# Attention and gated expert layer on one core: masks and identity made on the chip, byte-wise third words for ten weight blocks, a new written order, fills in the quieter bank

## The chip, the cores and the metric

The kernel runs on 1 core of one Trainium2 chip. The metric is the device time of one execution in microseconds (us); three executions are given for the kernel before, and one more was recorded by the profiler. Engines are named as the profile does: PE (TensorE matmul), PEld (its weight load), DVE (VectorE), ACT (ScalarE), POOL (GpSimd), SP (SyncE, which issues the DMAs here).

## The reference

```python
# attention: batch 4, heads 8, sequence 768, head size 64; block 32, window 16
k_sum = k.reshape(B, H, nb, block, D).max(axis=3)
v_sum = v.reshape(B, H, nb, block, D).mean(axis=3)
scores_l = scale * np.matmul(q, k.transpose(0, 1, 3, 2))
mask_l = np.abs(pos[:, None] - pos[None, :]) < window
scores_s = scale * np.einsum('bhsd,bhnd->bhsn', q, k_sum) + np.log(block)
scores_all = np.concatenate([np.where(mask_l, scores_l, -1e9), scores_s], axis=-1)
a = np.exp(scores_all - scores_all.max(-1, keepdims=True))
a = a / (a.sum(-1, keepdims=True) + 1e-9)
attn = np.matmul(a, np.concatenate([v, v_sum], axis=2))
# layer on x = attn, heads side by side: batch 4, sequence 768, width 512, inner width 1024
xk = mu_k * x + (1.0 - mu_k) * x_prev      # x_prev: x of the token before
xr = mu_r * x + (1.0 - mu_r) * x_prev
k = np.maximum(xk @ w_k, 0.0)
out = (1.0 / (1.0 + np.exp(-(xr @ w_r)))) * (k * k @ w_v)
```

The weights w_k, w_v and w_r come as 64-bit words (the inputs are 64-bit floats) and are turned into 32-bit floats on the chip; each is then kept as a high and a low part, and a product takes three matmuls (high by high, low by high, high by low).

## The kernel before

**Attention.** A "set" is one batch and one pair of heads (4 x 4 of them), a "unit" is half of the sequence of a set (32 units). `load_set` loads the keys (`kt`, L386; for the first set in two pieces) and the values (`vx`, L391), takes the maxima of key blocks (`kred` L412, `kmax` L416 and L420) and copies them between the windows of `kt` (`kcopy`, L424, on DVE or POOL). For the first batch the means of value blocks go through PE (`vpool` L436, `vsel` L444) and are spread into `vx` by POOL or DVE (`spread`, L450). `unit` loads a query tile (L465), makes the scores (24 small matmuls, L476), adds the mask and takes the minimum of the negated scores in one DVE operation (`mask`, L486, six a unit), takes the exponential (ACT, L490), adds 1e-9 (`eps`), takes the reciprocal, scales (`norm3`, L501 DVE, L507 ACT, L512 POOL), transposes by the identity (PE, L524), copies to SBUF (`pts`, L530 ACT, L532 DVE) and multiplies with the values (L539); the result is copied to `vx` (`evac`, L553 or L554).

**Layer.** `mixes` makes the two blends of a token with the one before and their high and low parts (`mixa` L572 or L575, `mixd` L579, `cast` or `khv` L582 or L584, `sub` L585). `gate` multiplies with w_r (L626 to L628) and takes the sigmoid. For the first half of the first batch it runs by pair of heads (`gate_p`, four operations of nine matmuls). `experts` has `e1` (L655, 12 matmuls for each of eight blocks), relu, square, the split in two parts, and `e2a` and `e2b` (L680, the last block at L706); L712 multiplies by the gate, L716 stores.

**Weights.** Twenty blocks (four of w_r, eight of w_k, eight of w_v), each of 512 KB. `load` (L320) brings the words into one of three `st` tiles; `wscale` (ACT, L327) turns the high words into a float pattern in one of four `wc` tiles; `wshift` (DVE, L331) shifts it left by 3; `wor` (DVE, L335) joins in the upper three bits of the low words; `wcast` (L344 ACT, L346 POOL, L348 DVE) makes the high part and `wsub` (DVE, L349) the low part.

**Constants.** One transfer (L288) brings `fixed_sb`: the three masks of 120 columns, the factors mu, two small selection matrices and the identity of 128 columns, 556 columns in all. `vpool`, `vsel`, the masks, the transposes and the blends all name it as a dependence.

**Order.** All work stands in a list of numbered operations. `ORDER`, a text of 1910 numbers with a letter where an operation goes to another engine than its usual one, says in which order they are issued; each engine works through its own part of that list strictly in turn, SP's queue of transfers too. `Plan.schedule` gives each a planned start from a table of durations (`LENGTH`) and a model of the transfers; these planned starts decide two things only: how many filling matmuls (L753, on a zero tile `still`, into the unused end of the `av` bank) stand ahead of a real PE operation, until the first e1 or gate, and on which DVE operation a POOL operation of the kinds in `SHARED` has to wait.

Of the kernel before, what the change touches and what calls it, by code (L numbers as in the profile page):

```python
# [9 lines left out]
F32 = mybir.dt.float32  # L10
F32R = mybir.dt.float32r
U32 = mybir.dt.uint32
AF = mybir.ActivationFunctionType
ALU = mybir.AluOpType
# [5 lines left out]
BLOCK, WINDOW = 32, 16  # L20
P = 128
# [11 lines left out]
NFIX = 3 * NK + 68 + P  # L33
# [5 lines left out]
LENGTH = dict(  # L39
    score=776, transpose=245, vtrans=30, vpool=800, vsel=320, values=848, mixe=1400, gate=2797, gate_p=2095, e1=2103,  # L40
    e2a=1398, e2b=700, e2=700, e2h=350,
    kred=862, kred2=460, kmax=75, kcopy=225, vred=865, mask=203, eps_d=72, rc=100, norm3=448, evac=470, pts_d=468,
    mixd=530, mixa_d=330, sub=471, psub=472, khv=271, spread=575, wshift=340, wor=605, wsub=605, wcast_d=340,
# [6 lines left out]
    "wor", "wsub", "mixd", "sub", "khv", "kcopy", "eps_d", "kmax", "spread", "wshift", "wcast_d", "norm3", "mixa_d", "diag_d",  # L50
# [5 lines left out]
DMA_FIRST, DMA_ISSUE, DMA_START, DMA_EACH, DMA_END, DMA_BYTES_PER_NS = 740, 470, 900, 100, 1200, 400.0  # L56
FIXED_MORE = 320000
# [5 lines left out]
SPLIT = 0  # L63
BY_PAIR = ((0, 0),)
# [8 lines left out]
245D 376P 399 57 286 246 265D 377 58 619 324 104 585 388 65 93 81 247D 282 278 280 288 266 284 59 60 248 378D 267D 400
82 398 83 379 66 94 269 289 281 279 287 268 74 250A 301 75 270 380 98 348 643 283 285 381 290D 76 271 389 77 78 675
272 84 403 401 308 291 310 302 306 382D 292D 312 309 383 304 105 95 402 404 273 294 325 275A 313 384 390 293 295 385
86 407D 386D 589 387 99 311 307 303 296 297 405 391 408 106 85 409D 107 87 305 108 298 128 586 406 410 314D 88 411 100
89 109 394 96 393 332 315 423 101 317P 328 116 110 412 129 330 334 326 336 413 102 130 316D 97 349 90 414A 318 91 117
416 415 392 319 299A 424 118 131 119 320 421 132P 354 652 759 761 140 594 134 701 588 417D 331 41 321 422 120D 355 337
322 352 590 121 418 335 103 430 111 141 329 419 358 420 112 360 333 327 323A 425 428 142 133 113 135 338 478P 587 122
431D 647 429 474P 350 356 437 339 114 357 479 340D 341D 115 359 426A 432 427 342 361 351 353 143 433A 434 136 435 152  # L80
343 123 436 144 591 362 137 344 363 595 164 345 364 346 145 606 124 598 125 365D 438 366 439 444 599 367D 347A 153
440A 482 602 604 600 126P 644 146 596 79 368 620 369 445 480 127 154 475 370 165 155 442 371A 156 481 483 157 158 677
443 486 441 484D 476 138 607 487 147 488 451 139 605 627 477 485 489 449 452 601 446 453 603 166 167 148 490 705 149
623 150D 631 159 496 597 447A 151 608D 160 450 456 609 161 491 1145 170 577 492 646 625 629 611P 617 454A 504P 500D
501 621 448 497 578 505 614 457 168 162 163 171 493 494 579 615 172 610 648 649P 580 653 495 169 173 763 506 581 735
702 575 612 654 507 656 658 664 791 508P 502 503 455 509 498 630 499 458 510 632 459 626 463 460 461A 624 613 174D 511
464 538 175 576 665 539 659 622 462 582 471 583 465 468 512 628 584 657 704 706 660 633D 634 472 469 517 592 762 466
636P 635D 662 513D 514 540 661 473 703 1149 639 708 1021 710 1023 593 760 650 616 678 515 663 618A 640D 655 839P 637
689 707P 685 709 470 1029 1019 645 768 764 516 679 518 524 522 683 687 666D 681 519 638D 667 817D 520A 521 818 669
819D 820 525D 711 641 672 523 529 722 673D 1022 718 765 840 684 690 686 541 526 688 668 670 527 1148 714 723 680 682  # L90
530 531 528 716 712 642 536 1025 1026 720 532 1033 841 715 671 651 533 545 717 534 721 719 713 535 691D 692 694 724
766 767 1063 1032 736 693D 674 1473 1031 1034 725 467 726P 733 695 676 537 696 737 741 739 738 740 727P 843 697 698D
1035 793 543 745 747 728 743 1150 844 842 546 821 699 742 542 769 700 729 730 1020 780 552 746 744 748 776 772 774
749D 778 547 770 777 731D 750 751D 794 752P 732 1087 553 1476 1088 1147 753 771 554 775 734 544 559 779 1024 1038 1465
795 796 754 845 822 823 781 773 825D 826 548 549 755 797 550 782 824 803 847P 551 801 783 784 560 756D 799 1477 804
798 800 557 555 805 846 1478 561 802 757 806 786 558 827 787 785D 758A 564 807D 808 1151 562 810 788 1039 789 848 556
790 918D 1048 828 813 1050 1091 563 809D 1040 565 919 1044 814 1467 1096 792A 829D 1051 569 566 572 811 1041 1046 1042
830 1090 831D 1064 812 832 815 1045 1043 1089 1205 1027 1049 837 1047 567 851D 849 852 1069 853D 854 1067 1073 1065
1052D 1074 1071 1053 835 570 1055 1028 1075 1054P 573 1237 1153 568 1037 1589 1030 1066 1072 1070 816A 850 1068 1092
1093P 855 1056 1097 1095 926 927 1057D 1058 1121 836 838 574 1211 867 833 1036 1076 1179 930 1108 1109 856 1593 1077D  # L100
1104 1100 1105 857 858 859 1592 834 1098 1078 1106 1079 1080D 1102 1059D 860 861D 1099 1122 862 1107 868D 1060 863 931
1103 869 1081 895 932 1061 1463 1154 1094 865 1125 1062A 1101 864 1082D 1110D 1111 1127 870 1083 866 928 872 896 1594
897 898 920 921 873 874 1112D 1126 1595 922 1128 1133 871 879 875 1129 1464 1123 923 933 880 888 1131 876 877 940 1469
1124 1132 1084D 899 924 941 889D 1130 1119 1155 1085 1212 1114 1177 1113 881 1115 929 878 944 882D 1134 1135 1116 886
1158 1156 925 1166 1167 883 1468 948D 949 934 884 1086A 1159 1157 1160 1204 1117 935 1203 1210 571 887 893 885 945 890
1648 894 891A 936 892 1162 1207 1136 1137 900 937 1164 1206 1208 1209P 1479P 938 1180 1165 942 939 943 1118 1507 1138D
952D 1470 1139 1120A 1146 901 902 1187 1191 953 954D 950D 946D 1235 951 1140D 1265D 947 907 903 904 905A 1188 1163
1141 908 906 1161 955 1287D 1288 1189 912 915 956 1289D 916 1183 1181 1261 1182 1266 1185 957 1142 1262 1267D 1268
# [751 lines left out]
```

## Time and profile before

| | us |
|---|---|
| median of three runs | 445.19 |
| lowest and highest | 444.62, 445.21 |
| the profiled execution | 445.36 |
| its span from the first to the last instruction | 443.6 |
| outside the span | 1.76 |

The profile is one execution. Its page gives the busy time of each engine, 40 slices of the span, the chain of work that ended last and the costliest groups of instructions. Matmuls are pipelined and overlap in the records, so a busy PE is not PE at its peak; the filling matmuls count as busy too. Instructions of DVE and ACT overlap their successors a little as well, so the distance between two starts is shorter than a duration.

### The profile page before, as it was taken

What the parts mean: (1) busy time and instruction counts of PE and PEld (TensorE: products, weight loads), DVE (VectorE), ACT (ScalarE), POOL (GpSimd) and SP (SyncE); (2) the same over time, 40 slices, a digit from 0 to 9 for tenths busy, and PEclk for the clock granted to TensorE, in tenths of its full rate; (3) what the DMA queues carried; (4) which work ended last, traced back from release to release, by engine and by line L of the source; (5) the groups of instructions that cost most, each with busy time, mean ns of one, the idle gap of its engine ahead of it and who ended that gap; (6) DMA issues with size and microseconds to landing.
All of it is one profiled execution on the core that took longest, in us unless ns stands there. A gap on an engine that the chain in (4) does not pass through costs nothing.

```text
span 443.6 us, 9603 instructions
## 1 busy us (share of the span) xinstructions
PE 436.4 (98%) x3582; PEld 375.6 (85%) x3582; DVE 297.1 (67%) x972; ACT 273.3 (62%) x807; POOL 30.9 (7%) x78
## 2 busy tenths in 40 slices
PE   7999999999999999999999999999999999999996
PEld 7877888889888888878898888888888888989885
DVE  3999989998998946648767755557643646444211
ACT  2999999885777597575466666564964315223321
POOL 0140211101030000000000210000000000000000
PEclk9999999999999999999999999999999999999999
DMA  8985868437656170141440143101200010002002
GB/s 309 401 299 194 281 249 265 149 126 227 228 141 253 55 239 27 53 153 55 134 144 19 44 117 105 51 1 42 79 1 1 2 47 1 0 1 95 0 1 95
DMA packets 26878, 51.95 MB, mean 117 GB/s; under 512 B 2512, under 2 KB 14416, under 8 KB 26832
## 3 DMA queue, kind: packets, MB, share of 16 engines
q1 hardware_dynamic: 26832, 51.35, 34.7%
q8 instruction: 28, 0.46, 0.5%
q14 instruction: 18, 0.15, 0.1%
HBM read 43.28 MB, written 6.29 MB: 112 GB/s over the span
## 4 chain that ended last, share of the span: by engine, by line
PE 87%; ACT 5%; DVE 3%; DMA 2%; issue 1%; SPq 0%; DVEq 0%; ACTq 0%
PE mm L655 28%; PE mm L680 25%; PE av L539 5%; PE pt L524 5%; PE sc L476 5%; PE mm L628 4%; PE mm L626 4%; PE mm L627 4%; PE mm L706 4%; PE av L753 2%; ACT y L490 2%; DMA st<-in_w_k 1%; DMA kt<-in_k 1%; DVE y L486 1%; ACT wc L327 1%
## 5 line engine op out<-in xcount | busy, mean ns | idle before, releaser
L655 PE MATMUL mm<-xs,wk_h 128*128 128x384 f32 x512 | 102.0, 341 | 0.6 <-DVE r L663 0.4
L655 PEld LDWEIGHTS mm<-xs,wk_h 128*128 128x128 f32 x512 | 89.5, 188 | 5.7 <-DVE r L663 1.1
L490 ACT ACTIVATE y<-y,mn 128x120 f32<-128x120 f32 x192 | 74.0, 387 | 31.0 <-DVE mn L486 30.8
L680 PE MATMUL mm<-wv_h,kh 128*128 128x512 f32 x168 | 67.2, 400 | 0.0
L680 PE MATMUL mm<-wv_l,kh 128*128 128x512 f32 x168 | 66.3, 395 | 0.0
L655 PE MATMUL mm<-xs,wk_l 128*128 128x384 f32 x256 | 55.3, 337 | 0.0
L665 ACT ACTIVATE r<-r 128x384 f32<-128x384 f32 x64 | 32.7, 520 | 35.0 <-DVE r L663 34.3
L670 DVE TENSOR_TENSOR kl<-r,kh 128x384 fp32r<-128x384 f32 x64 | 35.4, 559 | 26.7 <-ACT kh L669 18.9
L486 DVE CUSTOM_DVE_ANT_0 y<-sc,fixed_sb 128x120 f32<-128x120 f32 x192 | 47.4, 274 | 5.9 <-PE sc L476 3.7
L680 PE MATMUL mm<-wv_h,kl 128*128 128x512 f32 x168 | 49.7, 404 | 0.0
L661 ACT ACTIVATE r<-mm 128x384 f32<-128x384 f32 x42 | 20.5, 489 | 46.2 <-PE mm L655 41.6
L579 DVE SCALAR_TENSOR_TENSOR xa<-vx,fixed_sb,xa 128x384 f32<-128x384 f32 x64 | 39.1, 613 | 10.6 <-ACT xa L572 9.5
L655 PEld LDWEIGHTS mm<-xs,wk_l 128*128 128x128 f32 x256 | 45.6, 188 | 0.0
L585 DVE TENSOR_TENSOR xs<-xa,xs 128x384 fp32r<-128x384 f32 x64 | 35.1, 554 | 5.7 <-ACT xs L582 5.3
L626 PE MATMUL mm<-wr_h,xs 128*128 128x512 f32 x96 | 38.6, 402 | 0.0
L628 PE MATMUL mm<-wr_h,xs 128*128 128x512 f32 x96 | 38.0, 396 | 0.0
L627 PE MATMUL mm<-wr_l,xs 128*128 128x512 f32 x96 | 37.9, 395 | 0.0
L680 PEld LDWEIGHTS mm<-wv_h,kh 128*128 128x128 f32 x168 | 31.6, 188 | 6.2 <-DVE kh L668 0.3
L680 PEld LDWEIGHTS mm<-wv_l,kh 128*128 128x128 f32 x168 | 31.6, 188 | 6.0
L490 ACT ACTIVATION_READ_ACCUMULATOR y<-y,mn 128x1 f32 x192 | 36.3, 189 | 0.0
L680 PEld LDWEIGHTS mm<-wv_h,kl 128*128 128x128 f32 x168 | 30.2, 188 | 5.4
L524 PE MATMUL pt<-fixed_sb,y 128*120 128x128 f32 x192 | 33.2, 282 | 0.0
(76 smaller groups left out, 654.2 us busy)
## 6 DMA issues: line engine op xcount, KB each, us to landing
vx<-in_v SPq DMA_DIRECT2D x32, 384.0 KB
kt<-in_k SPq DMA_DIRECT2D x15, 544.0 KB
qt<-in_q SPq DMA_DIRECT2D x32, 192.0 KB
out<-z SPq DMA_DIRECT2D x23, 256.0 KB
st<-in_vT SPq DMA_DIRECT2D x12, 384.0 KB
st<-in_w_k SPq DMA_DIRECT2D x8, 512.0 KB
st<-in_w_v SPq DMA_DIRECT2D x8, 512.0 KB
st<-in_w_r SPq DMA_DIRECT2D x4, 512.0 KB
```

The source lines that it names most:

```text
L486: op("DVE", "mask", lambda h=h, i=i, var=var: nc.vector.tensor_tensor_reduce(out=y[h].t[:, i, :], in0=sc[h].t[:, i, 0:NK], in1=mask_sb[:, ...
L490: op("ACT", "exp", lambda h=h, i=i: nc.scalar.activation(y[h].t[:, i, :], y[h].t[:, i, :], AF.Exp, bias=mn[h].t[:, i:i + 1], scale=-1.0, a ...
L524: nc.tensor.transpose(out=pt.t[0:NK, i * P:(i + 1) * P], in_=y[h].t[:, i, :], identity=ident_sb)
L579: op("DVE", "mixd", lambda xt=xt, xa=xa, p=p: nc.vector.scalar_tensor_tensor(out=xa.t, in0=xt.t[:, 1 + lo:1 + lo + HT], scalar=mu_sb[:, wh ...
L585: op("DVE", "sub", lambda xa=xa, xh=xh, xl=xl: nc.vector.tensor_tensor(out=xl.t, in0=xa.t, in1=xh.t.bitcast(F32), op=ALU.subtract), reads= ...
L626: nc.tensor.matmul(ps[t].t, xh.t[:, ts], wr_h[:, p, :], start=(p == 0), stop=False)
L627: nc.tensor.matmul(ps[t].t, xh.t[:, ts], wr_l[:, p, :], start=False, stop=False)
L628: nc.tensor.matmul(ps[t].t, xl.t[:, ts], wr_h[:, p, :], start=False, stop=(p == NPAIR - 1))
L655: nc.tensor.matmul(ps.t[:, 0:HT], w[:, j, p, :], x[p][s].t, start=(n == 0), stop=(n == 11))
L665: op("ACT", "square", lambda: nc.scalar.activation(r.t, r.t, AF.Square), reads=[(r, 0)], writes=[(r, 0)])
L670: op("DVE", "sub", lambda: nc.vector.tensor_tensor(out=kl.t, in0=r.t, in1=kh.t.bitcast(F32), op=ALU.subtract), reads=[(r, 0), (kh, 0)], wr ...
L680: nc.tensor.matmul(acc[t].t, a.t[:, t * P:(t + 1) * P], w[:, j, :], start=start, stop=stop)
```

## The change

The transfer of constants shrinks from 556 to 76 columns (mu and the selection matrices, padded). The masks and the identity are made in place by five new operations: `plain` (DVE: two memsets, 360 columns and 3 x 24 columns), `band` (POOL: six `affine_select` on 64 partitions each, four of 3 x 64 columns and two of 3 x 32), `edges` (DVE: two memsets on 64 partitions), a memset of the identity tile (DVE) and `one` (POOL: one `affine_select` of 128 columns).

For ten of the twenty weight blocks (all of w_v, and blocks 2 and 3 of w_r) `wshift` goes away. A new operation `third` reads one byte of every low word, turns it into its upper three bits by one multiply and add with rounding, and writes it over the low word; `join` is then one DVE operation that shifts and joins, in the place of `wor`. `third` stands on POOL nine times and on ACT once.

`ORDER` is new as a whole (1915 numbers), and the transfer model and the table have other numbers and the kinds of the new operations. The filling matmuls now go to the bank of `av` or of `pt`, whichever was used less lately, and are left out where even that bank was in use until 300 ns before the end of the PE operation before.

Counted over the whole program, on DVE: `wshift` 20 to 10, `kcopy` 9 to 11, `norm3` 31 to 30, `pts` 33 to 22, `relu` 22 to 29, `eps` 22 to 9, `wcast` 4 to 7, `khv` 64 to 66, `mixa` 23 to 25, `evac` 9 to 11, `spread` 0 to 1. On ACT: `eps` 10 to 23, `norm3` 23 to 31, `pts` 31 to 42, `relu` 42 to 35, `wcast` 14 to 11, `cast` 64 to 62, `evac` 23 to 21, `mixa` 31 to 30, `third` 0 to 1. On POOL: `norm3` 10 to 3, `kcopy` 7 to 5, `spread` 8 to 7, `mixa` 10 to 9, `third` 0 to 9, `band` and `one`.

```diff
-NFIX = 3 * NK + 68 + P
+NFIX = 76
+FAR = -1.0e9 / 0.125
...
+THIRD = tuple(("wv", i) for i in range(8)) + (("wr", 2), ("wr", 3))
...
+    def plain():
+        nc.vector.memset(mask_sb, 0.0)
+        nc.vector.memset(mask_sb[:, :, QW:KB], float(np.float32(np.log(BLOCK)) / SCALE))
+    def band():
+        for c in range(2):
+            half = mask_sb[c * QW:(c + 1) * QW]
+            near, far = half[:, :, 0:QW], half[:, :, KB:NK]
+            for x, base, step in ((near, -1, 1), (near, 2 * WINDOW - 1, -1), (far, 2 * WINDOW - 1 - QW, -1)):
+                nc.gpsimd.affine_select(
+                    out=x, in_=x, pattern=[[0, 3], [step, x.shape[2]]], compare_op=ALU.is_ge, fill=FAR,
+                    base=base, channel_multiplier=-step)
+    def edges():
+        nc.vector.memset(mask_sb[0:QW, 0, 0:WINDOW], FAR)
+        nc.vector.memset(mask_sb[QW:P, 2, KB + WINDOW:NK], FAR)
+    def one():
+        nc.gpsimd.affine_select(
+            out=ident_sb, in_=ident_sb, pattern=[[-1, P]], compare_op=ALU.not_equal, fill=1.0, base=0, channel_multiplier=1)
+    op("DVE", "plain", plain, writes=MASK)
+    op("POOL", "band", band, reads=MASK, writes=MASK)
+    op("DVE", "edges", edges, reads=MASK, writes=MASK)
+    op("DVE", "edges", lambda: nc.vector.memset(ident_sb, 0.0), writes=IDENT)
+    op("POOL", "one", one, reads=IDENT, writes=IDENT)
...
+        def byte():
+            return st.t.bitcast(U8).rearrange("p (a b) -> p a b", b=8)[:, :, 3]
+        def third():
+            nc.scalar.activation(words()[1], byte(), AF.Copy, scale=1.0 / 32, bias=-31.0 / 64)
+        def third_other(eng):
+            return lambda: eng.tensor_scalar(
+                out=words()[1], in0=byte(), scalar1=1.0 / 32, scalar2=-31.0 / 64, op0=ALU.mult, op1=ALU.add)
+        def join():
+            nc.vector.scalar_tensor_tensor(
+                out=wc.t, in0=wc.t, scalar=3, in1=words()[1], op0=ALU.logical_shift_left, op1=ALU.bitwise_or)
...
-        op("DVE", "wshift", shift, reads=whole, writes=whole)
-        op("DVE", "wor", low, reads=[(st, 0), *whole], writes=whole)
+        if (name, i) in THIRD:
+            op("ACT", "third", third, reads=[(st, 0)], writes=[(st, 1)],
+               other=[("POOL", "third_p", third_other(nc.gpsimd)), ("DVE", "third_d", third_other(nc.vector))])
+            op("DVE", "wor", join, reads=[(st, 1), *whole], writes=whole)
+        else:
+            op("DVE", "wshift", shift, reads=whole, writes=whole)
+            op("DVE", "wor", low, reads=[(st, 0), *whole], writes=whole)
...
-            for _ in range(int(max(0, o.start - max(end, COLD)) // WARM + max(0, min(o.start, COLD) - end) // WARM_COLD)):
-                nc.tensor.matmul(spare, still, still, start=True, stop=True)
+            quiet = min(used, key=used.get)
+            many = int(max(0, o.start - max(end, COLD)) // WARM + max(0, min(o.start, COLD) - end) // WARM_COLD)
+            for _ in range(many if used[quiet] + 300 < end else 0):
+                nc.tensor.matmul(spare[quiet], still, still, start=True, stop=True)
```

What the new order says of the first stretch, engine by engine (before, then after):

```text
SP before: kt set01, kt set00 a, kt set00 b, q000, fixed, q010, wr0, wr1, wr2, vx00 x2, kt set02, kt set03, q020, vx01 x2, q030, wr3, vx02 x2, ...
SP after:  kt set00 a, kt set00 b, q000, fixed, kt set01, wr0, q010, wr1, vx00 x2, wr2, kt set02, kt set03, q020, vx01 x2, q030, vx02 x2, ... wr3 later
DVE before: kred set01, kred2 a, kmax, kred2 b, kmax x3, kcopy set00, kcopy set01, six masks of unit000, ...
DVE after:  plain, identity memset, kred2 a, kmax, kred2 b, kmax, edges, four masks of unit000, kmax, kred set01, two masks, kmax, wshift wr0, wor wr0, masks of unit010, ...
POOL before: spread set00, tiny, tiny, kcopy set02, ...
POOL after:  one, band, kcopy set00, kcopy set01, wcast wr0, third wr2, tiny, spread set00, ...
PE: the same twenty operations up to and with the first gate_p, with vpool set02 and values unit010 exchanged
```

## Rows read from the trace of the kernel before

**Rows 1.** The page, part 1: busy us, share of span, instructions of each engine.
```profile
PE 436.4 (98%) x3582; PEld 375.6 (85%) x3582; DVE 297.1 (67%) x972; ACT 273.3 (62%) x807; POOL 30.9 (7%) x78
```
**Rows 2.** Windows, all instructions: stretch, length, then PE, PEld, DVE, ACT, POOL, clock, DMA.
```profile
20.00:25.00 5.00, 5.00 (x101) 3.92 (x97) 4.48 (x24) 4.88 (x21) 2.00 (x5) 1.00 1.06 377
...
300.00:350.00 50.00, 50.00 (x372) 43.29 (x371) 27.07 (x89) 30.00 (x81) 1.05 (x3) 1.00 0.07 25
...
29.37:75.00 45.63, 44.94 (x466) 36.87 (x464) 43.78 (x144) 44.60 (x129) 8.57 (x13) 1.00 0.72 243
```
**Rows 3.** PE in order of time: start us, us, line, operation; the first stretch.
```profile
0.99 5.49 PE L753 MATMUL av<-still 128*128 128x128 f32 x32 [0.99 <-POOL still L747]
8.01 0.84 PE L476 MATMUL sc<-kt,qt 64*64 64x120 f32 x24 [1.53 <-DVE kt L424]
8.79 1.60 PE L753 MATMUL av<-still 128*128 128x128 f32 x12
10.32 0.85 PE L476 MATMUL sc<-kt,qt 64*64 64x120 f32 x24
...
29.37 0.47 PE L626 MATMUL mm<-wr_h,xs 128*128 128x512 f32 x1
```
**Rows 4.** The chain of waits in order of time: start us, us, what.
```profile
1.64 4.93 DMA kt<-in_k
...
7.64 0.32 DVE kt L424
...
27.37 0.47 DVE xs L585
```
**Rows 5.** Windows of half a us, all instructions (last column: GB/s moved).
```profile
2.50:3.00 0.50, 0.50 (x4) 0.50 (x4) 0.00 (x0) 0.00 (x0) 0.00 (x0) 1.00 0.99 400
...
4.50:5.00 0.50, 0.50 (x7) 0.50 (x6) 0.50 (x1) 0.00 (x0) 0.00 (x0) 1.00 0.82 226
```
**Rows 6.** DVE in order of time: start us, us; in brackets idle before.
```profile
4.13 1.42 DVE L412 TENSOR_REDUCE kg<-kt 128x48 f32<-128x768 f32 x2 [4.13 <-DMA kt<-in_k]
6.59 0.17 DVE L416 TENSOR_REDUCE kg<-kt 128x1 f32<-128x16 f32 x1 [1.04 <-DMA kt<-in_k]
...
8.92 0.28 DVE L486 CUSTOM_DVE_ANT_0 y<-sc,fixed_sb 128x120 f32<-128x120 f32 x1 [0.75 <-PE sc L476]
...
11.20 0.28 DVE L486 CUSTOM_DVE_ANT_0 y<-sc,fixed_sb 128x120 f32<-128x120 f32 x1 [0.97 <-PE sc L476]
...
27.30 0.54 DVE L585 TENSOR_TENSOR xs<-xa,xs 128x384 fp32r<-128x384 f32 x1
```
**Rows 7.** Groups of instructions by line and shape: busy us, mean ns.
```profile
L501 DVE TENSOR_TENSOR y<-y,rc 128x360 f32<-128x360 f32 x31 | 16.2, 525 | 0.1
...
L412 DVE TENSOR_REDUCE kg<-kt 128x48 f32<-128x768 f32 x15 | 14.2, 944 | 4.1 <-DMA kt<-in_k 4.1
...
L512 POOL TENSOR_SCALAR y<-y,rc 128x120 f32<-128x120 f32 x30 | 12.0, 415 | 143.4 <-DVE rc L498 71.3 <-ACT xs L582 64.6 <-ACT y L490 7.5
...
L584 DVE CAST xs<-xa 128x384 fp32r<-128x384 f32 x31 | 10.7, 357 | 3.9 <-PE mm L627 3.2 <-PE mm L628 0.6
...
L575 DVE TENSOR_SCALAR xa<-vx,om_sb 128x384 f32<-128x384 f32 x23 | 9.5, 418 | 0.0
...
L331 DVE TENSOR_SCALAR wc<-wc 128x512 uint32<-128x512 uint32 x20 | 8.3, 420 | 1.0 <-ACT wc L327 0.8
...
L346 POOL TENSOR_SCALAR wk_h<-wc 128x512 fp32r<-128x512 f32 x1 | 1.0, 992 | 3.9 <-DVE wc L335 3.9
```
**Rows 8.** POOL in order of time: start us, us; its first calls of three operations.
```profile
0.73 0.20 POOL L747 MEMSET still<- 128x128 f32 x1 [0.29 <-POOLq L849]
18.12 0.82 POOL L450 COPY vx<-vm 24x768 f32<-24x768 f32 x1 [17.18 <-ACT vm L446]
...
19.19 0.65 POOL L424 COPY kt<-ks 128x288 f32<-128x288 f32 x1
...
22.11 0.59 POOL L575 TENSOR_SCALAR xa<-vx,om_sb 128x384 f32<-128x384 f32 x1 [0.52 <-DMA vx<-in_v]
```

More of the change, by code (lines that the diff above doesn't have):

```diff
@@ L12 @@
 U32 = mybir.dt.uint32
+U8 = mybir.dt.uint8
 AF = mybir.ActivationFunctionType
@@ L39 @@
 LENGTH = dict(
+    plain=350, band=2700, edges=150, one=330,
     score=776, transpose=245, vtrans=30, vpool=800, vsel=320, values=848, mixe=1400, gate=2797, gate_p=2095, e1=2103,
@@ L42 @@
     kred=862, kred2=460, kmax=75, kcopy=225, vred=865, mask=203, eps_d=72, rc=100, norm3=448, evac=470, pts_d=468,
-    mixd=530, mixa_d=330, sub=471, psub=472, khv=271, spread=575, wshift=340, wor=605, wsub=605, wcast_d=340,
+    mixd=530, mixa_d=330, sub=471, psub=472, khv=271, spread=575, wshift=340, third_d=340, third_p=650, third=570, wor=605, wsub=605, wcast_d=340,
     diag_d=135, relu_d=468, result=605, resulth=341,
@@ L49 @@
 SHARED = (
-    "wor", "wsub", "mixd", "sub", "khv", "kcopy", "eps_d", "kmax", "spread", "wshift", "wcast_d", "norm3", "mixa_d", "diag_d",
+    "wor", "wsub", "mixd", "sub", "khv", "kcopy", "eps_d", "kmax", "spread", "wshift", "third_p", "third_d", "third", "wcast_d", "norm3", "mixa_d", "diag_d",
     "vzero", "vzero_d", "wcast_p", "mixa_p", "kcopy_p", "spread_p", "norm3_p",
@@ L73 @@
[L73 to L77, printed above, removed]
@@ L373, in block_means @@
             out=tp.t[0:NPAIR * NS, 0:P], in_=vs.t, identity=ident_sb),
-           reads=[(vs, p) for p in range(NPAIR)] + [*FIXED], writes=[(tp, 0)])
+           reads=[(vs, p) for p in range(NPAIR)] + [*IDENT], writes=[(tp, 0)])
         op("ACT", "vm", lambda: nc.scalar.activation(
@@ L488, in unit @@
                     op0=ALU.add, op1=ALU.min, accum_out=mn[h].t[:, i:i + 1]),
-                   reads=[(sc[h], 0), *FIXED], writes=[(y[h], i), (mn[h], i)])
+                   reads=[(sc[h], 0), *MASK], writes=[(y[h], i), (mn[h], i)])
                 op("ACT", "exp", lambda h=h, i=i: nc.scalar.activation(
@@ L527, in source @@
                 return pt.t[0:NK, 0:NSL * P].rearrange("p (i c) -> p i c", c=P)
-            op("PE", "transpose", turn, reads=[(y[h], i) for i in range(NSL)] + [*FIXED], writes=[(pt, 0)])
+            op("PE", "transpose", turn, reads=[(y[h], i) for i in range(NSL)] + [*IDENT], writes=[(pt, 0)])
             op("ACT", "pts", lambda h=h, source=source: nc.scalar.copy(out=pts[h].t, in_=source()),
@@ L814 @@
     vn = vn.reshape(B, NPAIR, P, 2, HW, P).transpose(0, 1, 3, 2, 4, 5)
-    i = np.arange(QW)[:, None]
-    j = np.arange(LK)[None, :]
-    near = np.abs(j - WINDOW - i) < WINDOW
-    mask = np.zeros((2, QW, 3, NK), np.float32)
-    for c in range(2):
-        for n, ok in enumerate((near & (j >= WINDOW) if c == 0 else near, near, near & (j < LK - WINDOW) if c else near)):
-            m = np.where(ok, 0.0, -1.0e9 / SCALE)
-            mask[c, :, n, 0:QW] = m[:, 0:QW]
-            mask[c, :, n, QW:KB] = np.float32(np.log(BLOCK)) / SCALE
-            mask[c, :, n, KB:NK] = m[:, QW:LK]
     mu = np.stack([np.asarray(inputs["moe_mu_k"]), np.asarray(inputs["moe_mu_r"])])
```

182 lines of the change are left out of this document (97 added, 85 removed).

## The prediction

> **What bounds the kernel now.** I read the page's engine shares first: PE is busy for 98% of the span, DVE 67%, ACT 62%, POOL 7% [rows 1]. Then the windows, to see whether that is one regime. It is two. From 300 to 350 us PE is busy all the time while DVE has 27 of 50 us and ACT 30; no work on DVE or ACT there can move the end. From 20 to 25 us DVE and ACT are nearly as full as PE [rows 2], and the operations of PE in order of time show why PE only looks full before that: its first 8 us are filling matmuls and a gap of 1.53 us, and fills, the first of 1.60 us, stand between the real operations after it [rows 3]. From the first gate product at 29.37 us on there are no fills, and of the 45.63 us up to 75 only 0.69 are idle [rows 3, 2]. So the kernel is a PE-bound stream that starts late: what PE could not do before 29.37 us is added to the end, one for one. The chain of waits says what makes it late: a transfer of keys until 6.57 us, then the copy of block maxima on DVE, and from 21.6 to 31 us DVE operations one behind the other, of which one stands there [rows 4]. Only that start can give time: the change has to bring forward the moment at which PE never waits again.
>
> **The first score.** Before, the first transfer is the 544 KB of set 01; DVE takes it up at 4.13 us, and the last piece of set 00 only at 6.59 us [rows 6]. After, the two pieces of set 00 (280 + 264 KB, the same 544 KB) go first, so I put their landing at 4.13 us too, and the first piece 264 KB / 0.4 MB per us = 0.7 us earlier [rows 5]. From the last landing to the copy DVE took 7.64 - 6.59 = 1.05 us [rows 6, 4], with one small operation of 0.15 us for set 01 among them: 0.9 us, so 5.03 us. The copy moves from DVE (0.32 us [rows 4]) to POOL (0.65 us in the first row of it [rows 8], plus some 0.15 us for the signal): score at 5.85 us instead of 8.01, and the first mask operation at 5.85 + 0.91 (before: 8.92 - 8.01) = 6.76 us: **2.16 us earlier**. Queries land behind the keys with 192 KB, 0.5 us more, still in time.
>
> **Is the mask there by then?** No row shows an affine_select. Nearest rows: a POOL operation of 120 columns takes 0.42 us, one of 288 columns at worst 0.65 us [rows 7, 8]; the pieces have 192 and 96 columns, so `band` is 6 x 0.42 = 2.5 to 6 x 0.65 = 3.9 us, `one` 0.42 to 0.65. They cannot start below the DVE memsets, which I put at 0.6 us by the 0.20 us for 128 columns [rows 8]: POOL begins at about 1.4 us, `band` ends between 4.3 and 5.95 us. The copy of set 00 is queued behind it on POOL, the masks behind `edges` on DVE. The copy is due at 5.05 us, so the price is 0 to 0.9 us, and less cannot be, because a faster `band` only waits. I take 0: the operation reads and writes one operand like the 0.42 row. DVE's memsets lie in its 4.13 us of waiting and are free.
>
> **DVE up to the first gate.** Between the first mask operation and the last DVE operation that this gate needs (27.30 us, handing on after 0.47 [rows 6, 4]) lie 18.85 us. A record of 0.54 us hands on after 0.47, so I take 0.08 off each record. The written orders differ there by: `kred` (0.86) and two `kmax` (0.08 each, by the 0.17 of rows 6) of set 01 moved behind the first masks, one `mixa` (0.34) and one `khv` (0.28) more; two `wshift` (0.34 each) and one `norm3` (0.45) fewer [rows 7]; two `eps` of six columns, also fewer, I leave out. Sum +0.5 us. DVE's waits in it: 0.97 us ahead of the second unit's masks [rows 6], in whose place stands a new one (`kmax` to POOL's copy to score 010, 1.8 us, of which the shift and join of wr0 cover 0.95), so -0.1. The gate's data are then 2.16 - 0.5 + 0.1 = 1.8 us earlier. The gate itself stood 1.6 us behind them, at 29.37 us, behind transposes and scores that stay ahead of it. **PE's full stretch starts 1.8 us earlier, at about 27.6 us**, with the same twenty PE operations done.
>
> **After that.** Up to the first e1, DVE's work is about as long as before (the same count of the two lists), and one more score stands ahead of e1 as ready work for PE. The other eight `wshift` take 8 x 0.34 = 2.7 us from DVE between 45 and 85 us, where it is full but PE hardly waits: worth at most the 0.69 us idle. I count **0.3**. ACT gets `eps`, `norm3` and `pts` in exchange for `relu` and casts; that load is priced with the rivals.
>
> **Third words.** Nine operations of 512 elements on POOL: 0.59 us (as for 384 columns) to 0.99 us each [rows 7, 8], 5.3 to 8.9 us on an engine that is idle for 93%. What counts is DVE behind a `join` that waits, wr2's above all, with the spread of set 00 queued behind that same POOL operation: 0 to 0.99 us, no gain possible. I take 0, since wr2 lands some two us before its `join` by the bytes ahead of it.
>
> **Transfers.** 240 KB less are 0.6 us at 400 GB/s [rows 5], and the queue is full until 25 us [rows 2]; w_r block 2 is moved behind the values of set 00, which land earlier by it. I count 0 of a gain of 0 to 0.6. Block 3 goes behind the weights of two e1; only the last of the four gate products needs it, and e1 work for PE stands right behind that one, so I count 0 there too.
>
> **Fills.** They cost where they outlast the wait: the 1.60 us of fills from 8.79 us stand ahead of a score for which the keys had been copied by 8.3 us, two copies of 0.32 us behind 7.64 [rows 3, 4]. With fewer of them, 0 to 1.5 us gained. The other side: fills stand four to half a us at 2.5 us and seven at 4.5 us, at a granted clock of 1.00 (2.4 GHz) in both windows [rows 5]; a stretch without fills could bring the slower pace back, and real work of 2 us at 4/7 of the pace would cost 1.5. The gap of 1.53 us before the first score is such a stretch, and 24 matmuls behind it took 0.84 us, against 0.85 for the next 24 [rows 3]: no sign of it. I count 0.
>
> **Sum.** 1.8 + 0.3 = 2.1 us off the profiled execution's 445.36 is 443.26; that execution is 0.17 above the median, so 443.1 us on the median's scale.
>
> **The rivals.** *Given back* (0.15): `band` ends at the upper bound (-0.9) and two joins wait for POOL (-0.5 each): 0.2 us left, 445.0; or ACT, nearly as full as DVE [rows 2], becomes the later of the two in the stretch that DVE is eased in. For it: POOL work now stands ahead of PE's first operation and of a DVE chain with hardly a gap. Against it: POOL is empty until 18.12 us [rows 8]. *POOL too late, slower* (0.09): the seven affine_selects take the 0.99 us of the slowest row [rows 7] each. `band` ends at 1.4 + 6.9 = 8.3 us, the copy at 9.1, the score 1.1 us later than before, and with +0.5 - 0.1 in DVE's list the gate is 1.5 us later than before, less the 0.3: 446.4. The point from which the 2.1 us are gone is `band` ending at 5.05 + 2.1 = 7.15 us, over 2.5 us later than I take. *More* (0.13): the fills' overrun (1.5) and the bubbles go too: 441.2. *Slower pace of PE* (0.04): 4.5 us of real work at 4/7 of the pace cost 3.4 us: 446.5. The rest, 0.59, is the forecast.
>
> The first calls of three POOL operations stand within 4 us of one another, with 0.82, 0.65 and 0.59 us [rows 8]: no room for anything long ahead of the second and third. The Trainium skill (GPSIMD Engine Reference, 2.1 Instruction dispatch) says that the first call of a freshly loaded kernel pays some 6 us for loading code, with no instruction in the profile. The rows speak against it for two of those, but affine_select is not among them; by that figure `band` would end 6 us later, the score come at about 11.2 us and the kernel take 448.5 us, an estimate by that page that belongs to the slower case.
>
> **How the numbers follow.** About 0.2% (0.9 us) is what a measurement of this kernel can tell from no change. Faster: 0.59 + 0.13 = 0.72; same 0.15; slower 0.13. The range goes from 440.9, the end of *more*, to 445.6, which takes in *given back* and leaves the slower cases out.
>
> **What would show it.** First score near 5.85 us and first mask operation near 6.8; affine_selects of 0.4 to 0.65 us, over before 5.05; first gate product near 27.6; no idle before the `join` operations; PE without gaps after that. I am wrong if `band` ends after 6 us, if DVE waits at a join, or if PE gets gaps between 28 and 75 us that it did not have.

## The result and the profile after

| | before | changed |
|---|---|---|
| median, us (lowest to highest, executions) | 445.19 | 441.1 (439.95 to 442.71, 5) |
| ratio of the times, 95% interval | | 0.9913 (0.9899 to 0.9927) |
| profiled execution, its span | 445.36, 443.57 | 439.95, 438.17 |
| first gate matmul | 29.37 | 27.07 |
| from there to the start of the last matmul | 410.04 | 406.91 |

The kernel became 4.1 us faster; 2.1 were forecast. The profiled execution is the fastest of its five; in a second set of executions the changed kernel had a median of 440.09. The last two rows of the table split the gain in the spans, 5.4 us: **2.30 us lie ahead of the first gate matmul and 3.13 us behind it**, where the forecast had 1.8 and 0.3.

The start went nearly as written. PE in order of time, of the changed kernel (start us, us, line, operation), as in [rows 3]:

```profile
5.81 0.84 PE L529 MATMUL sc<-kt,qt 64*64 64x120 f32 x24
6.58 3.17 PE L809 MATMUL av<-still 128*128 128x128 f32 x26
9.68 0.85 PE L529 MATMUL sc<-kt,qt 64*64 64x120 f32 x24
...
27.07 0.48 PE L679 MATMUL mm<-wr_h,xs 128*128 128x512 f32 x1
```

DVE in order of time, against [rows 6]: the memsets lie in its wait for the keys, and the first mask operation stands at 6.71 us.

```profile
0.88 0.36 DVE L298 MEMSET mask_sb<- 128x360 f32 x1 [0.88 <-PEq L897]
1.32 0.12 DVE L299 MEMSET mask_sb<- 128x72 f32 x1
1.42 0.17 DVE L321 MEMSET ident_sb<- 128x128 f32 x1
3.57 0.55 DVE L465 TENSOR_REDUCE kg<-kt 128x24 f32<-128x384 f32 x1 [1.99 <-DMA kt<-in_k]
...
6.71 0.28 DVE L539 CUSTOM_DVE_ANT_0 y<-sc,mask_sb 128x120 f32<-128x120 f32 x1 [1.45 <-PE sc L529]
```

POOL in order of time, against [rows 8]: seven affine_selects are over at 4.01 us, and POOL then waits 1.23 us before its copy.

```profile
1.66 0.29 POOL L315 TENSOR_SCALAR_AFFINE_SELECT ident_sb<-ident_sb 128x128 f32<-128x128 f32 x1 [0.72 <-DVE ident_sb L321]
1.89 0.10 POOL L600 MEMSET vx<- 128x1 f32 x1
1.94 2.07 POOL L306 TENSOR_SCALAR_AFFINE_SELECT mask_sb<-mask_sb 64x192 f32<-64x192 f32 x6
5.24 0.42 POOL L477 COPY kt<-ks 128x288 f32<-128x288 f32 x1 [1.23 <-DVE mask_sb L311]
...
14.11 0.79 POOL L375 TENSOR_SCALAR st<-st 128x512 uint32<-128x512 uint8 x1 [2.85 <-DVE wr_l L402]
```

The windows of the changed kernel, as in [rows 2] (stretch, length, then PE, PEld, DVE, ACT, POOL, clock, DMA), show the second part of the gain as something odd. In the 47.93 us from the first gate matmul to 75, PE is idle for 0.87 us, not less than the 0.69 before, and from 300 to 350 us it is busy without a break, as it was before.

```profile
27.07:75.00 47.93, 47.06 (x482) 39.81 (x481) 46.96 (x156) 47.55 (x141) 10.36 (x17) 1.00 0.75 257
300.00:350.00 50.00, 50.00 (x331) 43.57 (x331) 26.69 (x77) 26.19 (x74) 1.15 (x2) 1.00 0.09 31
```

So nothing waits less, and still the work behind the first gate matmul takes 3.1 us less. The answer is in the distance from one matmul to the next. The last gate product, first of the kernel before, then of the changed one (PE in order of time; six matmuls in a row, the first and the last):

```profile
437.43 0.40 PE L626 MATMUL mm<-wr_h,xs 128*128 128x512 f32 x1
...
438.59 0.40 PE L628 MATMUL mm<-wr_h,xs 128*128 128x512 f32 x1
```

```profile
432.02 0.39 PE L679 MATMUL mm<-wr_h,xs 128*128 128x512 f32 x1
...
433.16 0.39 PE L681 MATMUL mm<-wr_h,xs 128*128 128x512 f32 x1
```

Five distances take 1.16 us before and 1.14 after. Of the 784 pairs of neighbouring 512-column matmuls, 745 before and 746 after stand less than 300 ns apart; their mean distance is 232.7 ns before and 229.5 ns after, at a granted clock of 1.00 in both; 861 such matmuls x 3.2 ns are 2.8 us. The matmul of 384 columns hardly changed (177.8 and 177.4 ns).

### The profile page after: what moved, and what is told of

It is laid out like the page before. It is cut to its first block, busy times and chain, and to the rows that moved or that the text cites. A ratio compares the mean times of both kernels' runs of the same rounds, so it can differ in the third digit from the quotient of the medians.

```text
span 438.2 us, 9571 instructions
## 1 busy us (share of the span) xinstructions
PE 431.6 (99%) x3568; PEld 374.1 (85%) x3568; DVE 295.4 (67%) x961; ACT 277.9 (63%) x839; POOL 31.1 (7%) x69
## 4 chain that ended last, share of the span: by engine, by line
PE 80%; ACT 7%; DMA 5%; DVE 4%; SPq 1%; issue 1%; DVEq 0%
PE mm L708 27%; PE mm L733 24%; PE av L592 5%; PE pt L577 4%; PE mm L681 4%; PE mm L680 4%; PE mm L679 4%; PE sc L529 4%; PE mm L759 4%; DMA st<-in_w_k 3%; DMA kt<-in_k 2%; ACT wc L361 2%; ACT y L543 1%; DVE y L539 1%; ACT L693 1%
## 5 line engine op out<-in xcount | busy, mean ns | idle before, releaser
L539 DVE CUSTOM_DVE_ANT_0 y<-sc,mask_sb 128x120 f32<-128x120 f32 x192 | 46.8, 275 | 22.0 <-PE pt L577 17.6
L733 PE MATMUL mm<-wv_h,kl 128*128 128x512 f32 x168 | 48.7, 398 | 0.0
L716 DVE TENSOR_SCALAR r<-mm 128x384 f32<-128x384 f32 x29 | 16.1, 554 | 31.4 <-PE mm L708 29.6
L714 ACT ACTIVATE r<-mm 128x384 f32<-128x384 f32 x35 | 16.9, 485 | 30.1 <-PE mm L708 30.1
```

The lines of the kernel that those rows point to most:

```text
L539: op("DVE", "mask", lambda h=h, i=i, var=var: nc.vector.tensor_tensor_reduce(out=y[h].t[:, i, :], in0=sc[h].t[:, i, 0:NK], in1=mask_sb[:, ...
L733: nc.tensor.matmul(acc[t].t, a.t[:, t * P:(t + 1) * P], w[:, j, :], start=start, stop=stop)
```

## The experiments

Four theories. **Place**: the weights lie elsewhere in SBUF. The compiled kernel before lays `fixed_sb` (556 columns, 2224 bytes, rounded to 2240) and `om_sb` (32) ahead of `wk_h`, which begins at byte 140896 of its partition, 32 past a multiple of 64. After, it is 320 + 1440 + 512 + 32 bytes (mu, masks, identity, `om_sb`), and `wk_h` begins at 140928, a multiple of 64; `wv` and `wr` follow at multiples of 64 behind it. **Order**: the new order starts earlier and that is the gain; the new rule for the fills goes with it, for no run has it by itself. **Bytes**: ten `wshift` less on DVE are worth more than was counted. **Constants**: making masks and identity on the chip is the gain. Each run stands beside the kernel before on the same chip (medians 444.94 to 445.28; the first row of the table has one of them).

| run | median us (range, executions) | ratio to before | 512-column distance, ns | first gate, us | from there to the last matmul |
|---|---|---|---|---|---|
| before | 445.06 | | 232.7 | 29.37 | 410.04 |
| changed again | 440.09 (439.88 to 440.59, 4) | 0.9896 (0.9883 to 0.9909) | 229.6 | 27.47 | 406.80 |
| e1 before, weights at 64 | 442.85 (442.27 to 443.42, 5) | 0.9948 (0.9935 to 0.996) | 229.5 | 29.27 | 407.58 |
| e2 changed, weights at 32 | 442.47 (441.94 to 443.0, 5) | 0.9936 (0.9923 to 0.995) | 232.6 | 28.22 | 408.30 |
| e7 changed, 64 bytes further | 440.3 (439.27 to 441.17, 4) | 0.9898 (0.9885 to 0.9912) | 229.7 | 27.10 | 407.32 |
| e9 before, only wv and wr at 64 | 443.05 (442.27 to 443.56, 6) | 0.995 (0.9936 to 0.9964) | 229.1 | 28.69 | 408.07 |
| e10 before, only wk at 64 | 444.51 (444.01 to 446.18, 12) | 0.9988 (0.9978 to 0.9998) | 233.1 | 29.10 | 409.31 |
| e3 changed, constants transferred | 440.39 (439.49 to 441.53, 4) | 0.9892 (0.9874 to 0.9911) | 229.4 | 27.44 | 406.12 |
| e4 changed, no bytes | 442.71 (442.3 to 443.08, 5) | 0.9942 (0.993 to 0.9955) | 229.7 | 27.43 | 409.31 |
| e12 before, weights at 64, bytes | 443.59 (442.78 to 444.2, 7) | 0.9965 (0.9952 to 0.9979) | 229.3 | 29.90 | 407.72 |
| e8 new order alone, weights at 32 | 445.36 (444.18 to 446.68, 12) | 1.0008 (0.9998 to 1.0019) | 232.7 | 28.00 | 411.55 |
| e6 before, first keys first | 446.61 (445.88 to 446.94, 5) | 1.0038 (1.0026 to 1.005) | 232.7 | 31.04 | 409.92 |
| e11 changed, vx and y at 64 | 440.7 (439.87 to 441.05, 4) | 0.9895 (0.9879 to 0.991) | 229.5 | 27.58 | 406.91 |

The work from the first gate matmul on is the same in all of them, so the last column compares across rows.

**The changed kernel again**, unchanged, beside the second group of runs:

> The changed kernel as it is, beside the three runs of this call on one chip. Both theories: 440.5 to 441.8 us, 512-column matmuls 229.5 ns apart.

It came out as expected, at 440.09 us.

### The place of the weights

e1 is the kernel before with one unused tile, which moves the weights by 32 bytes and does nothing else:

```diff
     om_sb = const.tile([P, 2, NPAIR], F32, name="om_sb")
+    const.tile([P, 8], F32, name="pad_sb")
```

> The kernel before with one unused tile of 32 bytes a partition ahead of the weights, nothing else. Their place in SBUF moves from 32 to 0 modulo 64 bytes, which is their place in the changed kernel. Theory 'place': matmuls of 512 columns that read these weights as the moving operand follow each other at 229 to 230 ns (as in the changed kernel's profile) instead of 232.6, 861 of them, and those of 384 columns 1 ns closer: 2.5 to 3.2 us faster, 442.0 to 442.7 us. Rival 'execution': the pace of the changed kernel's profiled execution was that execution's own, so 445.0 to 445.4 us and 232.6 ns here.

442.85 us, 2.2 us off with not one instruction changed, a little less than the 2.5 to 3.2 expected. The last gate product of e1, to be set beside the two above:

```profile
434.90 0.39 PE L627 MATMUL mm<-wr_h,xs 128*128 128x512 f32 x1
...
436.04 0.39 PE L629 MATMUL mm<-wr_h,xs 128*128 128x512 f32 x1
```

1.14 us, as after. Since the two programs have the same order, the start of each matmul can be held against the start of the same matmul; the difference is small up to 90 us and then grows steadily to the end, as it does when every matmul of a kind is a little shorter:

```text
start in e1   start in before   difference, us
  7.91            8.01             0.10
 89.87           90.12             0.25
210.19          211.21             1.02
321.55          323.19             1.64
436.26          438.82             2.56
```

It is the reading of the weights, not the writing: their last part is written at 95.9 us in e1, and behind 100 us the distance is 229.3 ns there and 232.7 in the kernel before.

e2 is the reverse, the same line added to the changed kernel, so that its weights lie at 32 again:

> The changed kernel with one unused tile of 32 bytes a partition ahead of the weights, which puts them at 32 modulo 64 bytes, as in the kernel before. Theory 'place': 232.6 ns a matmul of 512 columns again, 2.5 to 3.2 us slower than the changed kernel's 441.1: 443.6 to 444.3 us; what is left of the gain is the earlier start, some 1 to 1.6 us below the kernel before's 445.2. Rival 'execution': 440.0 to 442.7 us as the changed kernel, with a pace that differs from run to run.

The distance went back to 232.6 ns. The time alone would not decide: 442.47 lies below the 443.6 to 444.3 of the theory and within the 440.0 to 442.7 of the rival. Against 440.09 and 441.1 the median is 1.4 to 2.4 us longer; from the first gate on it is 408.30 against 406.80 to 406.91, 1.4 to 1.5 us. The sign and the distance are settled, the size in this order less sharply than in e1.

e7 asks which multiple it has to be; the changed kernel with 64 unused bytes:

```diff
+    const.tile([P, 16], F32, name="pad_sb")
```

> The changed kernel with 64 unused bytes in each partition ahead of the weights, so that they begin 64 bytes past a multiple of 128. Theory 'a multiple of 64 bytes is enough': 512-column matmuls 229.5 ns apart and the time of the changed kernel on this chip within 0.4 us. Rival 'it has to be a multiple of 128 or more': 232.6 ns apart, 1.4 to 2.2 us slower.

229.7 ns and 440.3 us: a multiple of 64 is enough. e9 and e10 ask which side of the matmul counts. `wv` and `wr` are the moving side of their products (512 columns); `wk` is the stationary side of the first expert product, in which 384 columns of `xs` move, and `xs` did not change its place.

```diff
     wk_l = const.tile([P, NCV, NCK, P], F32R, name="wk_l")
+    const.tile([P, 8], F32, name="pad_sb")
```

> The kernel before with 32 unused bytes between wk_l and wv_h: wk stays 32 bytes past a multiple of 64 (it is the stationary side of the experts' first product, 384 columns of xs move), wv and wr begin at a multiple of 64 (512 columns of them move). Theory 'the moving side counts': 512-column matmuls 229.5 ns apart and 442.5 to 443.4 us, as with the padding ahead of wk. Rival 'both sides count': half or less of it, 443.8 to 444.7 us with 231 to 232.7 ns.

In e10 another such tile stands ahead of `wk_h` as well:

> The kernel before with 32 unused bytes ahead of wk_h and 32 behind wk_l: wk begins at a multiple of 64, wv and wr lie 32 bytes past one. Theory 'the moving side counts': no change, 444.7 to 445.4 us, 512-column matmuls 232.7 ns apart. Rival 'both sides count': 443.5 to 444.5 us.

e9 has the short distance (229.1 ns) and 443.05 us, the whole gain of e1; e10 has the long one (233.1). Its ratio, 0.9988 (0.9978 to 0.9998), leaves room for an effect of 0.1 to 1.0 us on the stationary side; 0.27 us of the profile's difference lie ahead of the first gate, and e9, with `wk` at 32, lost nothing against e1, so this stays open. **The moving side counts.** e11 lays the other tiles that stood at 32 at multiples of 64, every second one of the values and of the masked scores:

```diff
-        ... vx=tiles("vx", 10, [P, S + 1]),
+        ... vx=tiles("vx", 10, [P, S + 16]),
-        y=tiles("y", 4, [P, NSL, NK]), ...
+        y=[x[:, 0:NSL * NK].rearrange("p (n c) -> p n c", c=NK) for x in tiles("y", 4, [P, 368])], ...
```

> The changed kernel with the tiles of the values (vx) and of the masked scores (y) laid at multiples of 64 bytes each; every second one lies 32 bytes past one in the kernels before and after. They are the moving side of 720 short matmuls (64 columns) and the 174 transposes' stationary or moving side. Theory 'short matmuls are paced by something else': as the changed kernel, 439.8 to 441.2 us, the 720 matmuls 25.3 to 25.6 us together. Rival 'the place counts there too': up to 1 us less, 439.0 to 439.8 us, with the 720 at 24.5 to 25.2 us.

440.7 us, in the range of the first theory, but the run does not ask what its expectation says. In the kernel's calls `vx` is the stationary side of the short matmuls and `y` that of the transposes; the moving sides are `pts` and the identity, which stayed where they were. (`vx` moves only in the 96 matmuls of `vpool`.) The profile counts 768 short matmuls, and this line stands word for word in the answers for the changed kernel and for e11:

```profile
L592 PE MATMUL av<-pts,vx 120*64 120x64 f32 x768 | 29.4, 226 | 0.2 <-ACT vx L607 0.2
```

So no effect of the place of their stationary side shows; whether the place of a short moving tile counts was not tried. No version better than the changed kernel came of it.

### Order and bytes

e4 is the changed kernel without its bytes: the ten `third` are empty, and DVE does shift and join one behind the other where `join` stood. Order and weights' place stay.

```diff
-            op("DVE", "wor", join, reads=[(st, 1), *whole], writes=whole)
+            op("DVE", "wor", lambda: (shift(), low()), reads=[(st, 0), (st, 1), *whole], writes=whole)
```

> The changed kernel with the ten third-word operations left out on POOL and ACT and shift and join as two DVE operations in their place; all planned starts and the order unchanged. DVE gets ten times 0.34 us, two of them before the first gate product. Theory: 0.7 us at the start and up to 0.7 us in bubbles behind it: 441.8 to 442.5 us. Rival 'hidden': PE has work anyway, 441.1 us. Rival 'DVE sets the pace up to 85 us': all 3.4 us, 444.5 us.

442.71 us, a little above the 441.8 to 442.5 of the theory, 1.6 to 2.6 us above the changed kernel's two medians and 2.3 above e3, which ran beside it; it is close to the 442.85 of e1. So the new order without the bytes brings 0.1 us: it starts 1.84 us earlier than e1 (27.43 and 29.27) and gives 1.73 of it back behind the first gate (409.31 and 407.58). The trace says where: the answer for the tile `wv_l` of e4 up to 130 us (its writer's executions, what was idle until it came, and who waited; us, times).

```profile
L402 DVE TENSOR_TENSOR wv_l<-wc,wv_h x8: 683/685/690, 56.3 to 91.0; 128x512 fp32r<-128x512 f32 x8
...
  DVE wv_l L402: 2.2, 5
who waited for it (us, times):
  PEld mm L733: 1.8, 4
  PE mm L733: 0.4, 1
```

The same of the changed kernel: the writes are spread from 54.9 to 88.3 us, and nobody waits.

```profile
L402 DVE TENSOR_TENSOR wv_l<-wc,wv_h x8: 679/684/692, 54.9 to 88.3; 128x512 fp32r<-128x512 f32 x8
...
its engine sat idle before it (us, times) until:
who waited for it (us, times):
```

Matmul by matmul (same order in both; the changed kernel's second profile), e4 loses everything between 47 and 100 us and nothing after. Against its first profile the loss is 2.8 us, of which 0.4 lie ahead of 47 us:

```text
start in the changed kernel   in e4    difference, us
 53.85                         54.36      0.51
 65.04                         66.51      1.47
 76.58                         78.57      1.99
 97.59                        100.07      2.48
434.27                        436.74      2.47
```

e12 asks whether the bytes pay by themselves: the kernel before with e1's padding and its own order, in which POOL makes the ten blocks' bits right behind `wscale`, `wshift` is empty for them and `wor` is `join`.

```diff
-        op("ACT", "wscale", lift, reads=[(st, 0)], writes=whole)
-        op("DVE", "wshift", shift, reads=whole, writes=whole)
-        op("DVE", "wor", low, reads=[(st, 0), *whole], writes=whole)
+        op("ACT", "wscale", lambda: (lift(), third() if byte else None), reads=[(st, 0)], writes=whole)
+        op("DVE", "wshift", (lambda: None) if byte else shift, reads=whole, writes=whole)
+        op("DVE", "wor", join if byte else low, reads=[(st, 0), *whole], writes=whole)
```

> The kernel before with 32 unused bytes ahead of the weights (442.85 us by itself), its order of work kept, and the ten blocks' last three bits made by GpSimd from a byte, ahead of each block's join: ten shift instructions leave VectorE's list. Theory 'the bytes pay only because the new order asks for the weights earlier': TensorE waits for no weight in the old order (0.69 us idle in all), so 442.2 to 443.0 us, first gate matmul as before. Rival 'VectorE's ten shifts cost the same in any order': 1.6 to 2.6 us less, 440.2 to 441.3 us.

443.59 us, outside both ranges: not faster than e1 but 0.7 us slower. The first gate came 0.6 us later and the rest took 407.72 against 407.58. But the run did not ease DVE, which is what it was to test. First e1, then e12, from the first part of their pages:

```profile
PE 435.1 (99%) x3582; PEld 376.8 (85%) x3582; DVE 296.8 (67%) x972; ACT 273.3 (62%) x807; POOL 30.7 (7%) x78
```

```profile
PE 435.6 (99%) x3582; PEld 376.1 (85%) x3582; DVE 297.1 (67%) x962; ACT 273.8 (62%) x807; POOL 39.2 (9%) x88
```

DVE has ten operations less and is busy as long. In the changed kernel `third` stands in `SHARED`, so that on POOL it waits for a chosen DVE operation; in e12 it is issued inside `wscale` and has no such tie. That the tie makes the difference is inferred; no run takes away the tie alone. Nine DVE operations that ran beside one of the ten took 3.4 us longer together than the median of their kind; in the changed kernel two did, 0.7 us together (three and 0.9 in its second profile). One of the nine stands ahead of the first gate, in the second of two `mixd` (DVE in order of time, first e1, then e12), while POOL ran the byte operation L343:

```profile
23.22 1.20 DVE L580 SCALAR_TENSOR_TENSOR xa<-vx,fixed_sb,xa 128x384 f32<-128x384 f32 x2
```

```profile
23.50 1.60 DVE L592 SCALAR_TENSOR_TENSOR xa<-vx,fixed_sb,xa 128x384 f32<-128x384 f32 x2
```

POOL in order of time, of e1 and then of e12: the spread of values (L451, L463) waits in both. In e1 the profile names the masks on DVE; in e12 it names a transfer, but the mask operation of the same place is over at 25.50 us, just ahead of it. The spread did not stand behind L343, which was over 0.8 us before, and PE waits for it:

```profile
24.84 0.82 POOL L451 COPY vx<-vm 24x768 f32<-24x768 f32 x1 [1.21 <-DVE mn L487]
```

```profile
23.85 0.85 POOL L343 TENSOR_SCALAR st<-st 128x512 uint32<-128x512 uint8 x1
24.75 0.10 POOL L560 MEMSET vx<- 128x1 f32 x1
25.51 0.82 POOL L463 COPY vx<-vm 24x768 f32<-24x768 f32 x1 [0.67 <-DMA st<-in_w_k]
```

```profile
26.38 0.92 PE L552 MATMUL av<-pts,vx 120*64 120x64 f32 x24 [0.29 <-POOL vx L463]
```

Of the 0.6 us, 0.4 are that `mixd`; by the other 0.3, roughly, DVE was late before it. PE also waits 1.1 us for `wv_l` in this run. So with the weights at 64, the order alone gives 442.71, neither 442.85, and **both together 440.09**: the order brings nothing without the bytes. That the bytes bring nothing without the order is not shown, since e12 has them without the tie and did not ease DVE. What speaks for it is only that nobody waits for `wv_l` in e1.

e8 leaves only the new order: constants by transfer, no bytes, weights at 32.

> Of the change only the new order of work is left: masks and identity are transferred, every block's shift stands in VectorE's list with its join (no block takes its last three bits from a byte ahead of it), and the weights begin 32 bytes past a multiple of 64, as in the kernel before. Theory 'parts add up': 442.7 (shift in all blocks) plus 1.4 to 2.2 for the place of the weights, less 0 to 0.7 for the constants' engines' work: 443.4 to 444.9 us, 512-column matmuls 232.6 ns apart, first gate matmul at 27.4 to 28.2 us. Rival 'the order alone carries the whole gain': 441.0 to 442.0 us.

445.36 us, no gain, and above the 443.4 to 444.9 of *parts add up*: the parts do not quite add. The first gate was 1.4 us earlier and the rest 1.5 us longer, with 2.1 us of waits for `wv_l`. Of the 5.0 us between 445.06 and 440.09, the place is 2.2 (e1); the other 2.8 are what is left, in which the bytes count for 1.6 to 2.6 once the new order is there (e4), the constants for nothing that can be measured (e3, below), and the fills are not told apart. By the first set's 441.1 what is left is 1.7. The start of e8 also shows what the earlier start leans on (PE in order of time):

```profile
6.83 0.85 PE L505 MATMUL sc<-kt,qt 64*64 64x120 f32 x24 [0.78 <-DMA qt<-in_q]
```

Its first score waited for the query, which in the changed kernel was there. The landings scatter: with the new order, the first gate matmul lies between 27.07 and 28.22 us in eight profiles.

### The constants, and the first keys

e3 is the changed kernel with masks and identity transferred, in front of set 01's keys, and the five operations empty (a pad keeps the weights at 64):

```diff
-    op("DVE", "plain", plain, writes=MASK)
-    op("POOL", "band", band, reads=MASK, writes=MASK)
...
+    for eng, kind in (("DVE", "plain"), ("POOL", "band"), ("DVE", "edges"), ("DVE", "edges"), ("POOL", "one")):
+        op(eng, kind, lambda: None)
```

> The changed kernel with masks and identity brought by the one transfer of 278 KB again, and none of the five operations that make them; order, third words, planned starts and the place of the weights (0 modulo 64 bytes) as in the changed kernel. Theory: the transfer lands about 5.9 us, the first mask operation comes at 6.7, so only the 0.6 us of transfer time that all later loads get is at stake: 0 to 0.6 us slower, 441.1 to 441.7 us. Rival: making them on the chip is what carries the early start, then 1 to 2 us slower, 442 to 443 us.

440.39 us and a first gate at 27.44: no difference to the changed kernel that can be measured. The 240 KB that are no longer transferred bring nothing here; what the step brought came by the way, from where the weights slid to.

e6 is the kernel before with another start: set 00's keys lead SP's queue, and DVE's four steps on the keys of set 01 (`kred`, two `kmax`, `kcopy`; the expectation's "norm steps") follow the first masks (no padding, no bytes, planned transfer times without their extra).

```diff
-29 8 9 176 0 201 2 23 32 42 12 10 11 48 67 14 13 33 34 15 16 226 35 177 30 31 188 251 ...
+8 9 176 29 0 201 2 23 42 12 10 11 48 67 14 13 15 16 226 177 30 31 188 251 ... 32 33 34 35 202
```

> The kernel before with two things moved and no constants made on chip: the two key pieces of the first set lead SP's queue, and the four norm steps of the second set follow the first unit's masks on VectorE; the weights stay where they were in SBUF. Theory 'the order of transfers carries the start': first score at 5.8 to 6.4 us (8.01 before), first gate matmul 1.2 to 2.2 us earlier than 29.4, 512-column matmuls still 232.7 ns apart, time 443.0 to 443.9 us. Rival 'given back': the deferred norm steps and the later constants hold up the next unit; first gate matmul at 28.8 to 29.6 us, 444.6 to 445.4 us.

Both expectations failed; it is 1.55 us slower. DVE in order of time:

```profile
5.28 0.31 DVE L424 COPY kt<-ks 128x288 f32<-128x288 f32 x1
9.14 0.28 DVE L486 CUSTOM_DVE_ANT_0 y<-sc,fixed_sb 128x120 f32<-128x120 f32 x1 [3.55 <-DMA fixed_sb<-in_fixed]
```

The keys were ready at 5.6 us, but the masks still came by transfer, behind the 544 KB of set 01, and DVE sat idle for 3.55 us until they landed. The first gate moved to 31.04 us; from there on nothing changed (409.92). This is the waiting that putting the constants ahead of set 01 (e3), or making them on the chip, takes away; which of the two makes no difference.

## Why the prediction was right, and where it was not

The time lay in the range, near its lower end, and faster was the likeliest case. The forecast of 2.1 us was half of what came, and part of the reasoning behind it was wrong in a way that cancelled. That the time lay in the range is luck: the range reached down to 440.9 for *more*, which did not happen, and so it had room for 2.2 us from a cause that it does not name.

- **First score and masks: right.** 5.85 and 6.76 us forecast, 5.81 and 6.71 measured. The affine_selects took 0.29 us (128 columns) and 2.07 us for the six of the masks, 0.27 to 0.36 each, under the lower bound of 0.42, and were over at 4.01 us, ahead of the copy due at 5.05. The cost of 0 was right and *POOL too late* did not happen. The Trainium skill's 6 us for a first call (GPSIMD Engine Reference, 2.1 Instruction dispatch) is not seen in this trace: the first affine_select begins at 1.66 us, right behind the memset that it needs, and the second kind of them at 1.94, with 0.29 and 0.35 us.
- **First gate: right.** 27.6 us forecast, 27.07 and 27.47 in two profiles of the same kernel, within the scatter of landings (27.07 to 28.22 with the new order).
- **"What PE could not do before 29.37 us is added to the end, one for one": wrong by itself.** In e4 and e8, 1.84 and 1.4 us of earlier start were given back, 1.73 and 1.5 us, because the weights' low parts then came too late from DVE. That is the rival *given back* in kind, with DVE's weight work as its cause instead of `band`, the joins or ACT. It did not show because of the next point.
- **"Worth at most the 0.69 us idle": mis-sized.** The prediction worked out that eight `wshift` take 2.7 us from DVE between 45 and 85 us, and then capped their worth by PE's idle time before. Taking the bytes away cost 2.5 us (e4, matmul by matmul), against the 0.3 counted. The cap came from a trace in which PE reached that stretch 2 us later; an earlier PE needs DVE earlier by as much. PE's idle time is too small a measure besides: between 47 and 100 us it is 0.54 us in the changed kernel and 1.23 in e4, only 0.7 more for a loss of 2.5, because of the 2.2 us of waits for `wv_l` 1.8 stand at PEld, the weight load. In the trace before, though, nobody waits for `wv_l` at PEld either, so reading that engine alone would not have shown it.
- **Third words on POOL: nearly right.** They took 0.65 to 1.17 us, two of nine above the upper bound of 0.99, and 7.5 us together, inside the forecast. Two joins wait, 0.25 us (wr2's) and 0.18 us, where 0 was taken. Left out was that DVE operations beside them run longer: by 0.7 us in the changed kernel, where they are tied to DVE operations, and by 3.4 us in e12, where none is.
- **Transfers: right at 0** (e3), with a condition that the prediction did not name: the constants have to land ahead of the masks' first use (e6).
- **Fills: right at 0.** There are 98 instead of 112, all still in the `av` bank, with 3.17 us of them between the first two scores. No sign of a slower pace, at a granted clock of 1.00. *More* (441.2) met the time by other means than its own: the bubbles did not go (0.87 us idle up to 75 us), and the fills still stand there.
- **The place of the weights: not foreseen, 2.2 us.** The diff showed that `fixed_sb` shrinks and two tiles come in; the sum asked only what the transfer costs, not where the tiles behind them go.

So without the place of the weights the forecast would have been close (442.47 in e2, 443.1 forecast), but because two errors nearly cancelled: the start was counted in full though the order alone would have lost it, and the bytes at next to nothing though they are what keeps it. That, too, is luck.

## What to carry to other kernels

An earlier start of the bounding engine is worth its full length only if those who feed it are earlier too: for each feed of the stretch behind it, hold the time at which it is ready against the time at which it will now be asked for, and do not cap a saving by the idle time of the trace before. Read the waits of PEld beside the idle time of PE. When an experiment takes work from an engine, look first whether that engine's busy time fell, as it did not in e12. And when tiles change size, see where the tiles behind them slide to, and compare the distance of neighbouring matmuls before explaining a gain in a stretch where nothing waits.

## What the runs showed of the hardware

A matmul that moves 512 fp32r columns follows its predecessor after 229.1 to 229.7 ns when the moving tile begins at a multiple of 64 bytes of the partition and after 232.6 to 233.1 ns when it begins 32 bytes past one; an unused tile of 32 bytes was worth 2.2 us in 445. What in the chip makes the difference is open, and places other than these were not tried (0 and 64 bytes past a multiple of 128 gave the same, e7). The first affine_select, the only one of 128x128, took 0.29 us; those of 64x192 took 0.35 to 0.36, the first of them like the others. A DVE operation of two operands of 128x384 took 1.00 us in place of 0.61 while POOL turned 128x512 bytes into words (e12, 24.1 us).
